# Linear attention followed by a gated MLP: w_in loaded and cast by tiles of 128 or 256 rows, new orders for the first two batches, one PSUM bank per transpose and kv, softmax of the next chunk spread over more units

## Chip, cores, metric

The kernel runs on one core of one Trainium2 chip. The metric is the device time of one execution in microseconds (us). Times quoted as medians come from several executions; profiles show one execution each, whose "span" is about 1.8 us shorter than its time. All executions named here are in the fast state unless said otherwise (slow means over 1.5% above the fastest execution of the same kernel; unknown, that there was a single one). A ratio is the mean time of one kernel's fast runs over that of the other's of the same rounds, so it is not quite the ratio of the medians quoted beside it.

Four engines matter: TensorE (PE in the profile, its weight loads PEld), VectorE (DVE), ScalarE (ACT) and GpSimd (POOL). In this kernel each works off its own list in the order of the program, and semaphores make it wait for the others. The order of the calls in the source is therefore the schedule.

## The reference

```python
# q, k, v: [8 batches, 8 heads, 576 tokens, 64]
q_s = softmax(q, axis=-1)                      # over the 64 features of a head
k_s = softmax(k, axis=2)                       # over the 576 tokens
kv  = einsum('bhsd,bhse->bhde', k_s, v)        # 64x64 per head
x   = einsum('bhsd,bhde->bhse', q_s, kv)       # -> [8*576, 512]
h   = x @ w_in                                 # w_in [512, 2048]
g   = h * sigmoid(beta * h)
out = g @ w_out                                # w_out [2048, 512]
```

## The kernel before

The tokens are worked on in nine chunks of 512: the first 512 tokens of each of the eight batches, and one chunk made of the eight tails of 64. A chunk has 16 "units" `j`, one for each 128 of the 2048 hidden columns. A unit is four h matmuls (one for each 128 rows of w_in, `kt`), a tanh on ScalarE, a multiply on VectorE that makes g, and four acc matmuls, all of 128x512. The attention of a batch is worked on in four pairs of heads. A pair has a kv (TensorE), a division by the sum of the exps of k (the "norm", VectorE, tile kvp), transposes of q (tp, copied to qsT), x (TensorE) and a copy of x as bfloat16 (xT). TensorE's results go to buffers called PSUM banks, and the program lets a bank be written again once its reader is done. While TensorE works on chunk n, the function `side` slips the softmax of chunk n+1 in between its units. The first two batches are ordered by hand, line by line.

```python
    EB = 2
    w_in_b = [const.tile([P, KT, 2 * P], BF16, name=f"w_in_b{hh}") for hh in range(2 * EB)]
    w_in_c = {blk: const.tile([P, KT, 4, P], BF16, name=f"w_in_c{blk}") for blk in range(EB, 4)}
    ...
    def w_cast(kind, blk, half, eng):              # float32 staging tile -> bf16
        t = wst[kind, blk]
        if kind == "in":
            if blk >= EB:                          # blocks 2 and 3: sorted while cast
                c = slice(2 * half, 2 * half + 2)
                evac(eng, w_in_c[blk][:, c], t[:, c, :].rearrange("p kt (q e) -> p kt e q", e=4))
                return
            dst = w_in_b[2 * blk + half][:]        # blocks 0 and 1: plain
            src = t[:, :, half * 256 : half * 256 + 256]
        ...
    def hpe(c, j, kts, tag="h"):                   # the h matmuls of unit j
        if (c, j) not in h_of:                     # a PSUM bank; "h" takes b2 and b3 in turn
            h_of[c, j] = ps.tile([P, MAIN], F32, tag=bank(tag), bufs=1, name=f"h{c}_{j}")
        ...
    def mm_a(c, j, tag=None):
        hpe(c, j, range(KT), tag or "h")
        th_act(c, j)
        g_dve(c, j)                                # frees the bank of h
```

Each partition reads two (blocks 0, 1) or four (blocks 2, 3) neighbouring rows of w_out, so unit j owns every second or every fourth column of w_in. In blocks 0 and 1 the weight load of TensorE picks every second column. In blocks 2 and 3 the cast does the picking: it reads a float32 every 16 bytes.

```python
    def side(n, u):                                # softmax of the next chunk, unit u
        ...
        o = 2 if n == 1 else 0
        if u in (2 + o, 3 + o):
            q_exp(qc, u - 2 - o)                   # ScalarE, one half of q
            q_sum(qc, u - 2 - o)                   # VectorE: row sum, reciprocal
        if u in (4 + o, 5 + o):
            q_mul(qc, u - 4 - o)                   # VectorE
            if kb < B:
                k_exp(kb, u - 4 - o)               # ScalarE
        ...
        if u == 6 + o:
            if kb < B:
                ktail_exp(kb)
            q_xbar(qc)                             # transpose by DMA
        ...                                        # kv at 9, x at 11 to 14
    for n in range(1, NCH):
        c = order[n]
        for j in range(LEAD if n == 1 else 0, NJ):
            if not (n > 1 and j == 3):
                mm_a(c, j, ...)
            if n > 1 and j == 2:
                mm_a(c, 3)                         # units 2 and 3 back to back
            ...
                mm_b(c, j - LAG)                   # acc matmuls two units later
            side(n, j)
```

(The start of batch 0, the loads and the stores are left out here.)

The softmax here doesn't subtract the row's maximum and nothing guards it: scores larger than these inputs give would overflow.

## Time and profile before

| | before |
|---|---|
| time, median of 4 runs | 287.56 us (287.34 to 288.11) |
| span of the profiled run | 285.8 us |
| TensorE busy | 277.2 us, 97% |
| first h matmul | 16.36 us |
| step from chunk to chunk | 29.51 us |

The kernel is bound by TensorE. In the steady part a 128x512 matmul starts every 0.216 us, the figure that the Trainium skill ("TensorE: Matmul & The Clock Gate", section "Wait — 56ns, not 53.3ns?") gives for a warm array, 215.7 ns. The timeline of TensorE shows the waits of the head. Columns: start and duration in us, engine, line, operation, output and inputs, count; in brackets the idle time before it and what ended it.

```profile
16.36 7.07 PE L420 MATMUL h<-xT,w_in_b 128*128 128x512 bf16 x31
23.27 3.62 PE L468 MATMUL acc<-w_out_b,g 128*128 128x512 bf16 x16
27.39 3.63 PE L420 MATMUL h<-xT,w_in_c 128*128 128x512 bf16 x16 [0.51 <-POOL w_in_c L162]
30.86 3.62 PE L468 MATMUL acc<-w_out_b,g 128*128 128x512 bf16 x15
34.70 3.63 PE L420 MATMUL h<-xT,w_in_c 128*128 128x512 bf16 x16 [0.22 <-DVE rq L238]
```

Sixteen matmuls at 0.216 us take 3.45 us, so from 23.27 the next group could start at 26.72, and from 30.86 at 34.31. It started at 27.39 and 34.70. The casts of w_in blocks 2 and 3 are in the timelines of ScalarE and GpSimd:

```profile
25.26 2.06 ACT L160 CAST w_in_c<-w_in 128x1024 bf16<-128x1024 f32 x1 [0.44 <-DMA w_in<-in_moe_w_in_dram]
25.29 2.05 POOL L162 CAST w_in_c<-w_in 128x1024 bf16<-128x1024 f32 x1 [2.94 <-DMA w_in<-in_moe_w_in_dram]
...
30.60 4.04 POOL L162 CAST w_in_c<-w_in 128x1024 bf16<-128x1024 f32 x2 [1.68 <-DMA w_in<-in_moe_w_in_dram]
```

They end at 27.34 and at 34.64. The second wait was put down to VectorE by the profile (the reciprocal that ended nearest), but the GpSimd cast ends just as near, and h reads its result. The costliest groups show how slow these casts are for their size:

```profile
L162 POOL CAST w_in_c<-w_in 128x1024 bf16<-128x1024 f32 x3 | 6.1, 2047 | 4.6 <-DMA w_in<-in_moe_w_in_dram 4.6
L162 POOL CAST w_out_b<-w_out 128x1024 bf16<-128x1024 f32 x6 | 6.2, 1041 | 3.2 <-DMA w_out<-in_moe_w_out_dram 3.2
```

The same number of elements on the same engine takes 2047 ns with a 16-byte step and 1041 ns without. "SBUF — State Buffer" in the Trainium skill (section "Door 1: The DMA port swizzle", the note on cachelines) says that a line is 16 bytes and that an access pays when it crosses to a new one; at a step of four float32 every access does. The trace agrees, on ScalarE too (2.06 against 1.03 us).

One stretch of the steady part, timeline of all engines (weight loads and transfers left out), shows a wait that I overlooked when I predicted:

```profile
83.55 1.22 DVE L237 TENSOR_REDUCE rq<-eq 128x16 f32<-128x1024 bf16 x1 [0.26 <-ACT eq L226]
84.47 0.69 ACT L430 ACTIVATE th<-h,beta_t 128x512 bf16<-128x512 f32 x1
84.97 1.16 DVE L237 TENSOR_REDUCE rq<-eq 128x16 f32<-128x1024 bf16 x1
...
86.00 1.03 PE L468 MATMUL acc<-w_out_b,g 128*128 128x512 bf16 x4
86.34 0.63 DVE L434 SCALAR_TENSOR_TENSOR g<-th,h 128x512 bf16<-128x512 bf16 x1
...
87.02 1.02 PE L420 MATMUL h<-xT,w_in_b 128*128 128x512 bf16 x4
```

The acc group at 86.00 should be followed by h at 86.86; h comes at 87.02, 0.16 us late, and the line shows no idle time because matmuls overlap in the trace. The h of unit 6 needs the bank of unit 4, which g of unit 4 frees. Its tanh was ready at 85.16, but VectorE did two row sums first and ended g at 86.97.

### The profile page before, as it was taken

To read this page: it belongs to the slowest core of one execution; us is meant where nothing else is said; L and a number is where in the kernel's file an instruction comes from. 1 tells how busy PE (TensorE), PEld (TensorE's weight loads), DVE (VectorE), ACT (ScalarE), POOL (GpSimd) and SP (SyncE) were. 2 spreads that over 40 slices of the span, in tenths; PEclk is the share of its full clock that TensorE was granted. 3 is DMA by queue.
4 is the path that set the end of the run, shared out by engine and by line. 5 is a ranking of instruction groups with operands and counts; after the bars stand their busy time and mean duration, and the time that the engine had idled before them with its cause. 6 is when DMAs were issued, how large, how long until landed. Compare 5 with 4: busy or idle time off the path is not lost.

```text
span 285.8 us, 4292 instructions
## 1 busy us (share of the span) xinstructions
PE 277.2 (97%) x1655; PEld 130.2 (46%) x1684; DVE 178.0 (62%) x279; ACT 164.3 (57%) x238; POOL 42.9 (15%) x58
## 2 busy tenths in 40 slices
PE   8799999999999999999999999999999999999995
PEld 3453445444444444444444444444445444445543
DVE  4863777595478457854694569546964596445361
ACT  4687773683486448734783468355934564554451
POOL 6445682120030012000300030002100000000000
PEclk9999999999999999999999999999999999999999
DMA  6999999908942973099219912796371033005003
GB/s 213 383 372 394 385 395 320 291 10 222 310 167 49 310 193 144 14 275 270 97 52 260 284 51 106 149 244 160 149 178 45 1 147 73 2 0 147 2 0 147
DMA packets 55760, 50.09 MB, mean 175 GB/s; under 512 B 26294, under 2 KB 49082, under 8 KB 55612
## 3 DMA queue, kind: packets, MB, share of 16 engines
q1 hardware_dynamic: 55596, 49.69, 57.5%
q8 instruction: 13, 0.21, 0.3%
q10 hardware_dynamic: 144, 0.13, 0.1%
q14 instruction: 7, 0.06, 0.1%
HBM read 36.71 MB, written 9.44 MB: 161 GB/s over the span
## 4 chain that ended last, share of the span: by engine, by line
PE 85%; DMA 9%; DVE 1%; SPq 1%; ACT 1%; issue 1%; POOL 0%
PE h L420 40%; PE acc L468 39%; DMA q_st<-in_q_dram 4%; DMA k_st<-in_k_dram 3%; DMA w_in<-in_moe_w_in_dram 3%; PE x L370 2%; PE kv L330 2%; PE acc L460 1%; SPq L115 1%; DVE g L434 1%; PE kv L289 1%; DVE rq L237 0%; POOL w_in_b L162 0%; ACT eq L226 0%; PE tp L274 0%
## 5 line engine op out<-in xcount | busy, mean ns | idle before, releaser
L434 DVE SCALAR_TENSOR_TENSOR g<-th,h 128x512 bf16<-128x512 bf16 x144 | 97.8, 683 | 87.4 <-ACT th L430 86.0
L430 ACT ACTIVATE th<-h,beta_t 128x512 bf16<-128x512 f32 x144 | 98.5, 688 | 93.4 <-PE h L420 90.8
L468 PE MATMUL acc<-w_out_b,g 128*128 128x512 bf16 x547 | 138.9, 379 | 0.6 <-issue 0.2
L468 PEld LDWEIGHTS <-g 128*128 128x128 bf16 x560 | 54.6, 98 | 65.5 <-DVE g L434 0.5
L420 PE MATMUL h<-xT,w_in_c 128*128 128x512 bf16 x280 | 71.8, 379 | 1.1 <-POOL w_in_c L162 0.5
L420 PE MATMUL h<-xT,w_in_b 128*128 128x512 bf16 x281 | 70.9, 379 | 0.6
L420 PEld LDWEIGHTS <-w_in_b 128*128 128x128 bf16 x288 | 28.1, 98 | 33.9 <-issue 1.6
L420 PEld LDWEIGHTS <-w_in_c 128*128 128x128 bf16 x288 | 27.2, 98 | 32.6 <-POOL w_in_c L162 1.7
L162 POOL CAST va<-v_st 128x576 bf16<-128x576 f32 (+1 forms) x14 | 18.6, 1328 | 145.7 <-DMA v_st<-in_v_dram 145.6
L237 DVE TENSOR_REDUCE rq<-eq 128x16 f32<-128x1024 bf16 x18 | 21.6, 1199 | 5.9 <-ACT eq L226 5.9
L243 DVE TENSOR_TENSOR eq<-eq,rq 128x1024 bf16<-128x1024 bf16 x18 | 22.2, 1235 | 0.1
L226 ACT ACTIVATE eq<-q_st 128x1024 bf16<-128x1024 f32 x16 | 16.3, 1049 | 5.2 <-DMA q_st<-in_q_dram 5.2
L160 ACT COPY o<-acc 128x512 f32<-128x512 f32 (+1 forms) x18 | 9.6, 575 | 8.9 <-PE acc L468 6.0
L162 DVE COPY o<-acc 128x512 f32<-128x512 f32 (+1 forms) x19 | 12.1, 670 | 3.4 <-PE acc L468 3.2
L162 DVE CAST xT<-x 128x512 bf16<-128x512 f32 x19 | 13.0, 685 | 0.7 <-PE x L370 0.7
L160 ACT CAST xT<-x 128x512 bf16<-128x512 f32 x17 | 9.9, 587 | 6.1 <-PE x L370 5.3
L181 ACT ACTIVATE ek<-k_st 128x1024 bf16<-128x1024 f32 x12 | 12.6, 1047 | 0.0
L370 PE MATMUL x<-qsT,kvp 128*128 128x512 bf16 x32 | 12.0, 380 | 0.0
L541 PE MATMUL warm<-kvp 128*128 128x512 bf16 x29 | 8.9, 468 | 1.2 <-DVE kvp L630 1.2
L162 POOL CAST w_in_c<-w_in 128x1024 bf16<-128x1024 f32 x3 | 6.1, 2047 | 4.6 <-DMA w_in<-in_moe_w_in_dram 4.6
L162 POOL CAST w_out_b<-w_out 128x1024 bf16<-128x1024 f32 x6 | 6.2, 1041 | 3.2 <-DMA w_out<-in_moe_w_out_dram 3.2
L174 ACT ACTIVATE ek<-k_st 128x576 bf16<-128x576 f32 x8 | 5.5, 681 | 2.0 <-DMA k_st<-in_k_dram 1.9
(49 smaller groups left out, 93.9 us busy)
## 6 DMA issues: line engine op xcount, KB each, us to landing
out_dram<-o SPq DMA_DIRECT2D x14, 512.0 KB, 3.4
q_st<-in_q_dram SPq DMA_DIRECT2D x6, 1024.0 KB, 6.8
k_st<-in_k_dram SPq DMA_DIRECT2D x6, 1024.0 KB, 7.6
v_st<-in_v_dram SPq DMA_DIRECT2D x6, 1024.0 KB, 11.0
k_st<-in_k_dram SPq DMA_DIRECT2D x8, 288.0 KB, 7.8
v_st<-in_v_dram SPq DMA_DIRECT2D x8, 288.0 KB, 7.5
q_st<-in_q_dram SPq DMA_DIRECT2D x4, 512.0 KB, 8.7
w_in<-in_moe_w_in_dram SPq DMA_DIRECT2D x4, 512.0 KB, 6.8
```

The costliest lines, as they stand in the source:

```text
L160: eng.copy(dst, src)
L162: eng.tensor_copy(dst, src)
L181: nc.scalar.activation(ek[b][:, :, h, :].rearrange("p i h d -> p h i d"), k_st[b][:, h, 0 : R * D].rearrange("p h (i d) -> p h i d", i=R), ...
L226: nc.scalar.activation(eq[b][:, :, s * m : (s + 1) * m, :].rearrange("p i h d -> p h i d"), q_st[b][:, s * m : (s + 1) * m, :].rearrange(" ...
L237: nc.vector.tensor_reduce(rq[b][:, 0, :, h], eq[b][:, :, h, :], axis=AX.X, op=ALU.add)
L243: eng.tensor_tensor(eq[b][:, :, h, :], eq[b][:, :, h, :], rq[b][:, 1, :, h].unsqueeze(3).to_broadcast((P, R, m, D)), ALU.mult,)
L370: nc.tensor.matmul(t[:], kvp[:, c, j, :], qsT[c][:, :, j, :])
L420: nc.tensor.matmul(h[:], w_in_u[j // 2][:, kt, j % 2, :] if j < 4 * EB else w_in_c[j // 4][:, kt, j % 4, :], x_of(c)[:, kt, :], start=(kt ...
L430: nc.scalar.activation(th[:], h_of[c, j][:], ACTF.Tanh, scale=beta_t[:, j : j + 1])
L434: nc.vector.scalar_tensor_tensor(out=g[:], in0=th_of.pop((c, j))[:], scalar=1.0, in1=h_of[c, j][:], op0=ALU.add, op1=ALU.mult)
L468: nc.tensor.matmul(acc[st][:], g[:, ds(st * P, P)], w_out_b[:, j, :], start=(j == 0), stop=(j == NJ - 1),)
L541: nc.tensor.matmul(t[:], kvp[:, B - 1, 0, :], kvp[:, B - 1, :, :].rearrange("p j r -> p (j r)"))
```

## The change

Its intent: let the first h matmuls start earlier and shorten the last chain of the attention of batch 0 (one PSUM bank per pair, casts split over two engines, beta early), cast w_in without the slow step, and spread the softmax of the next chunk so that it does not stand in front of tanh and g. The core of the diff, with cuts:

```diff
-    w_in_b = [const.tile([P, KT, 2 * P], BF16, name=f"w_in_b{hh}") for hh in range(2 * EB)]
-    w_in_c = {blk: const.tile([P, KT, 4, P], BF16, name=f"w_in_c{blk}") for blk in range(EB, 4)}
+    w_in_b = [
+        [const.tile([P, n, 4 * P], BF16, name=f"w_in_b{blk}_{i}") for i in range(KT // n)]
+        for blk, n in enumerate((1, 1, 1, 2))
+    ]
 ...
+    def w_unit(j, kt):
+        t = w_in_b[j // 4]
+        n = KT // len(t)
+        return t[kt // n][:, kt % n, :].rearrange("p (hh q e) -> p hh e q", hh=2, e=2)[:, j % 4 // 2, j % 2, :]
 ...
-    def vz_cast(b, j, eng, m=1):
+    def vz_cast(b, j, eng, m=1, part=None):        # part: 5/9 on GpSimd, 4/9 on ScalarE
 ...
-    def w_castk(blk, half, kh, eng):
-        c = slice(2 * kh, 2 * kh + 2)
-        evac(eng, w_in_b[2 * blk + half][:, c, :], wst["in", blk][:, c, half * 256 : half * 256 + 256])
+    def w_castk(blk, kt, eng):
+        evac(eng, w_in_b[blk][kt][:, 0, :], wst["in", blk][:, kt, :])
 ...                                               # loads of batch 0 in a new order, then
     w_load("in", 0, 0)                             # four row tiles of 256 KB, were two column halves
     w_load("in", 0, 1)
+    w_load("in", 0, 2)
+    w_load("in", 0, 3)
 ...                                               # both hand-written orders replaced, in side:
-        o = 2 if n == 1 else 0
-        if u in (2 + o, 3 + o):
-            q_exp(qc, u - 2 - o)
-            q_sum(qc, u - 2 - o)
-        if u in (4 + o, 5 + o):
-            q_mul(qc, u - 4 - o)
+        w = u
+        if w == 2:
+            q_exp(qc, 0)
+            q_sum(qc, 0)
+        if w == 3:
+            q_exp(qc, 1)
+        if w == 4:
+            q_sum(qc, 1)
             if kb < B:
-                k_exp(kb, u - 4 - o)
+                k_exp(kb, 0)
 ...
+        if w == 5:
+            q_mul(qc, 0)
             if kb < B:
                 ktail_exp(kb)
+        if w == 6:
+            if kb < B:
+                k_exp(kb, 1)
+        if w == 7:
+            q_mul(qc, 1)
             q_xbar(qc)
```

## The prediction

> **What bounds the kernel now.** TensorE. The busy table gives PE 277.2 of 285.8 us (97%), clock 0.999. In the timeline of chunks 2 to 7 a 128x512 matmul starts every 0.216 us (four in 0.86 us, as the Trainium skill's "TensorE: Matmul & The Clock Gate" states for a warm array, 215.7 ns), and the chain of waits repeats every 29.51 us with about 0.1 us of "issue". 128 h/acc matmuls, 4 x and 0.76 us of kv add to 29.2 us, so nothing is to be won there. Only the head can give: (a) the first h matmul starts at 16.36 us; until then PE has warm matmuls, waits and small attention work; (b) from 16.36 to 49.3 us (batch 0 done) the PE timeline shows gaps of 0.51 (waiting for the POOL cast of w_in_c), 0.22, 0.16 us and smaller, about 1.25 us against 31.7 us of work. The tail is not touched. The DMA engines are saturated (share 1.0 and more, 370 to 396 GB/s) from 5 to 45 us.
>
> **What the change does.**
> 1. w_in block 0 arrives in four 256 KB row tiles (about 0.7 us each at 380 GB/s) instead of two 512 KB column halves. The first half landed at 15.03 and its two casts (0.62 us) ended at 15.68. With the last v tile still landing at about 13.5, row tile 0 lands at about 14.2 and is cast by 14.9; kt 0 of four j runs at once, and each next tile brings 0.86 us of PE work per 0.7 us of DMA.
> 2. Each kv pair has its own bank, so pair 0's x is done early; the last pair's chain is v cast split over ACT and POOL (0.67 us to about 0.4), kv 0.45, norm 0.65, x, eviction 0.6. Beta's work leaves the end of this chain for the start, where its issue (0.3 to 0.4 us) should be absorbed.
> 3. w_in blocks 2 and 3: the old casts read with a 16-byte step, 2.05 us per 128x1024 on ACT and POOL, while w_out's contiguous ones take 1.04. "SBUF — State Buffer" (cachelines of 16 bytes) explains such a factor; the trace agrees. New ones should take 0.62 per 128x512: 3.5 us of engine time saved, on the path only as the 0.51 us gap. The de-interleaving moves to the weight loads, which took 98 ns both ways.
> 4. Batch 1: last loads are k and v instead of w_out; chained by hand, PE stays the bound until 47.7 us.
> 5. Softmax spread: PE did not wait for it; about 0, perhaps 0.2 us at the start of chunk 1.
>
> **Sum.** Start of h: about 1.1 us (8 h matmuls done by 16.95 instead of 18.1). Gaps of chunk 0: about 0.5 of 1.25. Chunk 1: 0.1. Total 1.7 us of 287.5.
>
> **Predicted 285.8 us, 80% range 284.6 to 287.2. Faster by over 2%: 0.02; within 2%: 0.965; slower by over 2%: 0.015.**
>
> **What would show it.** First h matmul at 14.7 to 15.3 us with x of pair 3 after it; no 2.05 us w_in casts; no gap at "POOL w_in" near 27 us; the acc matmuls of batch 0 end about 1.6 us earlier; chunk period unchanged at 29.5 us; tail unchanged.
>
> **What would make it wrong.** Landings of v and w_in that shift with the order; in-order blocking on ACT, where casts that wait for a landing stand before tanh; the DVE chain of three norms and two evictions holding up kt 1 and 2; batch-2 loads not landed when chunk 1, without its two-unit delay, wants them.

## The result

| | before | after |
|---|---|---|
| time, median of 4 runs | 287.56 us | 286.0 us (285.58 to 286.44) |
| ratio of fast runs | | 0.9943, 95% interval 0.9921 to 0.9966 |
| span of the profiled run | 285.8 us | 283.9 us |
| first h matmul | 16.36 us | 16.36 us |
| first acc matmul of batch 0 | 23.27 us | 23.48 us |
| h of units 8 and on, batch 0 | 27.39 us | 26.94 us |
| h of units 12 and on, batch 0 | 34.70 us | 33.84 us |
| batch 0 done, two h matmuls of chunk 1 done | 49.31 us | 48.45 us |
| double h group of chunk 2 | 79.96 us | 79.10 us |
| double h group of the last chunk | 256.25 us | 254.43 us |
| last 24 acc matmuls | 275.26 us | 273.44 us |

The predicted 285.8 us was 0.2 us off. But the rows of the table do not agree with the way in which it was reached. In these two profiles the start of h did not move; the head lost 0.21 us up to the first acc matmul (the x of the last pair, one matmul, now comes after the first three h matmuls and not before them), then won 1.07 us up to 33.84, then nothing more; and the steady part, from which nothing was expected, won 0.96 us between chunk 2 and the last chunk. One predicted sign is there only on its face: the acc matmuls of batch 0 end about 1.5 us earlier (47.8 instead of 49.3 us), but three matmuls of chunk 1 that used to come before the last of them now come after it. Like for like, the gain there is 0.86 us.

Timeline of TensorE, after:

```profile
16.36 0.81 PE L422 MATMUL h<-xT,w_in_b 128*128 128x512 bf16 x3
...
17.23 6.42 PE L422 MATMUL h<-xT,w_in_b 128*128 128x512 bf16 x29
23.48 3.62 PE L470 MATMUL acc<-w_out_b,g 128*128 128x512 bf16 x16
26.94 3.62 PE L422 MATMUL h<-xT,w_in_b 128*128 128x512 bf16 x16
...
33.84 1.03 PE L422 MATMUL h<-xT,w_in_b 128*128 128x512 bf16 x4
```

The first three h matmuls are followed by x of the last pair, then by the other 29. From 17.23 us on nothing waits: 23.48 plus 3.45 is 26.93. The casts, in the timeline of GpSimd, end well ahead of their readers:

```profile
24.91 0.61 POOL L158 CAST w_in_b<-w_in 128x512 bf16<-128x512 f32 x1 [0.17 <-DMA w_in<-in_moe_w_in_dram]
...
31.71 1.04 POOL L158 CAST w_in_b<-w_in 128x1024 bf16<-128x1024 f32 x1 [3.14 <-DMA w_in<-in_moe_w_in_dram]
```

And the stretch of the steady part, timeline of all engines, after. Now g of unit 4 stands between the two row sums (84.34), and h of unit 6 follows its acc group without a gap (85.14 plus 0.86 is 86.00):

```profile
82.69 1.22 DVE L234 TENSOR_REDUCE rq<-eq 128x16 f32<-128x1024 bf16 x1 [0.26 <-ACT eq L223]
...
84.34 0.69 DVE L436 SCALAR_TENSOR_TENSOR g<-th,h 128x512 bf16<-128x512 bf16 x1
84.94 1.21 DVE L234 TENSOR_REDUCE rq<-eq 128x16 f32<-128x1024 bf16 x1
85.14 1.03 PE L470 MATMUL acc<-w_out_b,g 128*128 128x512 bf16 x4
...
86.01 1.03 PE L422 MATMUL h<-xT,w_in_b 128*128 128x512 bf16 x4
```

The chain of waits of the profile after, in order of time, says what the first h matmul waited for (start, duration, what):

```profile
2.12 5.64 DMA v_st<-in_v_dram
...
9.54 0.75 PE warm L543 x3
...
10.55 0.76 DVE qsT L158 x2
11.34 1.23 DVE rq L234
...
13.39 1.21 DVE eq L240
...
15.64 0.24 DVE kvp L304
15.92 0.60 PE x L370 x2
```

It starts with the landing of the first v tile, goes through the first kv, beta's transposes and three dummy matmuls ("warm") on TensorE, and from 10.55 us on it lies on VectorE, up to x and h. It is not w_in: the first row tile of w_in was cast by about 15.5 us.

### The profile page after: what moved, and what is told of

It reads as the page before. It is cut to its first block, busy times and chain, and to the rows that moved or that the text cites. A ratio compares the mean times of both kernels' runs of the same rounds, so it can differ in the third digit from the quotient of the medians.

```text
span 283.9 us, 4325 instructions
## 1 busy us (share of the span) xinstructions
PE 278.1 (98%) x1683; PEld 130.5 (46%) x1683; DVE 179.6 (63%) x285; ACT 164.4 (58%) x241; POOL 37.8 (13%) x59
## 4 chain that ended last, share of the span: by engine, by line
PE 94%; DMA 2%; DVE 2%; SPq 0%; POOL 0%; issue 0%; ACT 0%; POOLq 0%
PE h L422 44%; PE acc L470 43%; PE x L370 2%; DMA v_st<-in_v_dram 2%; PE kv L330 2%; PE acc L462 1%; PE kv L289 1%; DVE rq L234 0%; DVE eq L240 0%; PE tp L270 0%; PE x L374 0%; DVE kvp L304 0%; POOL va L158 0%; DVE qsT L158 0%; PE warm L543 0%
## 5 line engine op out<-in xcount | busy, mean ns | idle before, releaser
L422 PE MATMUL h<-xT,w_in_b 128*128 128x512 bf16 x576 | 144.0, 379 | 0.0
L470 PE MATMUL acc<-w_out_b,g 128*128 128x512 bf16 x560 | 140.8, 379 | 0.0
L422 PEld LDWEIGHTS <-w_in_b 128*128 128x128 bf16 x576 | 55.5, 98 | 63.9
L158 POOL CAST va<-v_st 128x320 bf16<-128x320 f32 (+2 forms) x14 | 16.7, 1192 | 150.0 <-DMA v_st<-in_v_dram 150.0
L543 PE MATMUL warm<-kvp 128*128 128x512 bf16 x33 | 10.3, 465 | 1.2 <-DVE kvp L627 1.2
L158 POOL CAST w_in_b<-w_in 128x512 bf16<-128x512 f32 (+1 forms) x11 | 6.9, 650 | 6.4 <-DMA w_in<-in_moe_w_in_dram 6.4
L543 PEld LDWEIGHTS <-kvp 128*128 128x128 bf16 x33 | 3.6, 116 | 6.4 <-issue 3.6
L330 PEld LDWEIGHTS <-ek 128*64 128x64 bf16 x192 | 4.1, 111 | 2.5 <-ACT th L432 2.5
L363 DVE TENSOR_TENSOR kvp<-kv,rk 64x256 bf16<-64x256 f32 x12 | 5.1, 422 | 0.3
## 6 DMA issues: line engine op xcount, KB each, us to landing
v_st<-in_v_dram SPq DMA_DIRECT2D x6, 1024.0 KB, 10.7
```

The source lines that it names most:

```text
L158: eng.tensor_copy(dst, src)
L422: nc.tensor.matmul(h[:], w_unit(j, kt), x_of(c)[:, kt, :], start=(kt == 0), stop=(kt == KT - 1),)
L470: nc.tensor.matmul(acc[st][:], g[:, ds(st * P, P)], w_out_b[:, j, :], start=(j == 0), stop=(j == NJ - 1),)
L543: nc.tensor.matmul(t[:], kvp[:, B - 1, 0, :], kvp[:, B - 1, :, :].rearrange("p j r -> p (j r)"))
```

## The experiments

Three theories follow from this. C: the slow casts caused both waits of the head. S: the two row sums in a row cost 0.16 us in each of six chunks. V: the head waits for the VectorE chain. The rival of C is that the new orders and banks gave the gain (O), the rival of S is the prediction (P).

### Softmax placement put back, and alone

The changed kernel with the body of `side` of the old one, and the reverse:

```diff
# e1_new_old_side: in the changed kernel (shortened; compare the diff above)
-        if w == 2: ... q_exp(qc, 0), q_sum(qc, 0)
-        ...
-        if w == 7: ... q_mul(qc, 1), q_xbar(qc)
+        o = 2 if n == 1 else 0
+        if u in (2 + o, 3 + o): ... q_exp, q_sum
+        ...
+        if u == 6 + o: ... ktail_exp, q_xbar
# e2_old_new_side: the reverse, in the old kernel
```

> The changed kernel with the old placement of the next chunk's softmax put back. Theory S (the spread of the softmax takes away a wait of 0.16 us in each of chunks 2 to 7, where the second row sum stands before g of unit 4 on VectorE and holds back the bank of h of unit 6): the step from chunk to chunk goes from 29.35 back to 29.51 us, the first 48 us stay, the span grows from 283.9 by about 1.0 to 284.9 us. Rival P (the prediction on record: TensorE did not wait for the softmax): span within 0.2 us of 283.9.

Measured: 286.9 us (median of 6), ratio to the old kernel 0.9974 (0.996 to 0.9987), profiled span 284.8 us. The double h groups of chunks 2 and 3, timeline of TensorE:

```profile
78.99 1.89 PE L422 MATMUL h<-xT,w_in_b 128*128 128x512 bf16 x8
108.51 1.89 PE L422 MATMUL h<-xT,w_in_b 128*128 128x512 bf16 x8
```

The step is back to 29.51 us (29.52 between these two rounded starts, 29.51 between the next), and the head is as in the changed kernel (first h at 16.26). S is right, P is wrong.

> The old kernel with only the new placement of the softmax. Theory S: chunk step 29.35 us instead of 29.51, span 285.8 - 1.0 = 284.8 us, with the first 49 us unchanged. Rival P: 285.6 to 285.8 us.

Measured: 286.35 us, ratio 0.9962 (0.9942 to 0.9981). The profiled span is only 285.4 us, but that profile is of one of the two longest of its six executions (287.18 us, still a fast run), and its head ran 0.58 us later than the old kernel's. The steps are what was to be tested:

```profile
80.54 1.89 PE L420 MATMUL h<-xT,w_in_b 128*128 128x512 bf16 x8
109.89 1.89 PE L420 MATMUL h<-xT,w_in_b 128*128 128x512 bf16 x8
```

The step is 29.35 us, and from chunk 2 to the last chunk 175.33 us (80.54 to 255.87) against 176.29 us before. The placement gives the 0.96 us by itself.

### Which half of the placement

Only the VectorE part, and only the ScalarE part, in the old kernel (one run each, so their state is unknown and their times are not compared):

```diff
# e3_old_dve_part
-            q_sum(qc, u - 2 - o)
-        if u in (4 + o, 5 + o):
-            q_mul(qc, u - 4 - o)
+        if u in (2 + o, 4 + o):
+            q_sum(qc, (u - 2 - o) // 2)
+        if u in (5 + o, 7 + o):
+            q_mul(qc, (u - 5 - o) // 2)
# and q_xbar at 7 + o instead of 6 + o
# e4_old_act_part
-            if kb < B:
-                k_exp(kb, u - 4 - o)
+        if u in (4 + o, 6 + o):
+            if kb < B:
+                k_exp(kb, (u - 4 - o) // 2)
# and ktail_exp at 5 + o instead of 6 + o
```

> The old kernel with only the VectorE half of the new placement: second row sum two units after the first, multiplies at units 5 and 7, transpose at 7; the exps of k on ScalarE stay. If the wait is VectorE's (g of unit 4 behind the second row sum), the chunk step falls from 29.51 to 29.35 us. If it was ScalarE's (tanh behind four exps), it stays at 29.51.

> The old kernel with only the ScalarE half: the second exp of k two units after the first, the tail's exp between them; the row sums and multiplies on VectorE stay. VectorE theory: chunk step stays at 29.51 us. ScalarE theory: 29.35 us.

Measured: steps of 29.35 us in the first (83.96 to 113.31 us) and 29.51 us in the second (80.38 to 109.89). The wait was VectorE's alone. (The first kernel moves the multiplies and the transpose too. That the row sum is what counted is read from the profile of before: only it stands in the list between the tanh and g of unit 4.) But the first kernel took 290.6 us, longer than before, for a reason that I had not expected. Its timeline of TensorE in chunk 1:

```profile
68.76 1.03 PE L468 MATMUL acc<-w_out_b,g 128*128 128x512 bf16 x4
72.74 0.38 PE L370 MATMUL x<-qsT,kvp 128*128 128x512 bf16 x1 [2.96 <-DMA qsT<-eq]
```

I had kept the old delay of two units in chunk 1 (`o`), so the transpose by DMA was issued at unit 9, after the last multiply, and x of unit 11 waited for it. The transpose took 5.4 us from issue to landing in that chunk. The changed kernel drops the delay, which is why it can multiply as late as unit 7. A part of a change that looks idle can be what makes another part harmless.

The second kernel showed something else about the old casts:

```profile
27.68 3.63 PE L420 MATMUL h<-xT,w_in_c 128*128 128x512 bf16 x16 [1.33 <-POOL w_in_c L162]
```

Here h had started at 15.64 us, 0.7 earlier than in the profile of before, and TensorE simply waited longer (1.33 us instead of 0.51) for the cast. With the slow casts the start of h is not what sets the pace of the head.

### Contiguous casts alone, and both parts together

```diff
# e5_old_contig: in the old kernel
-    EB = 2
+    EB = 4                                # all blocks laid out as blocks 0 and 1
-    beta_q = const.tile([4 - EB, 4 * P], F32, name="beta_q")
-    nc.sync.dma_start(beta_q[:], ...)     # and its four small transposes and its copy
# e6_old_contig_new_side: the same, and the new body of side
```

> The old kernel with w_in blocks 2 and 3 cast without the 16-byte step (and w_out and beta laid out to match), its orders and its loads of w_in kept. Theory C (the slow casts alone caused both waits of TensorE near 27 and 34.5 us): the casts of 128x1024 take about 1.05 us instead of 2.05; the first h matmul stays at 16.3 to 16.4 us; the h groups that started at 27.39 and 34.70 us start at about 26.9 and 33.8; span about 0.9 shorter, 284.9 us. Rival O (the new orders and banks of the head gave the gain): the waits change only by 0.5 us or less in all, span 285.3 or more.

Measured: 286.18 us, ratio 0.9952 (0.994 to 0.9965), span 284.4 us. The timeline of GpSimd and that of TensorE:

```profile
24.97 1.04 POOL L161 CAST w_in_b<-w_in 128x1024 bf16<-128x1024 f32 x1 [2.95 <-DMA w_in<-in_moe_w_in_dram]
...
30.25 2.03 POOL L161 CAST w_in_b<-w_in 128x1024 bf16<-128x1024 f32 x2 [1.67 <-DMA w_in<-in_moe_w_in_dram]
```

```profile
15.81 7.07 PE L419 MATMUL h<-xT,w_in_b 128*128 128x512 bf16 x32
...
26.17 3.62 PE L419 MATMUL h<-xT,w_in_b 128*128 128x512 bf16 x16
...
33.08 3.62 PE L419 MATMUL h<-xT,w_in_b 128*128 128x512 bf16 x16
```

Both waits are gone, with the old orders kept: h of units 8 and 12 starts 10.36 and 17.27 us after the first h matmul, against 11.03 and 18.34 us before, and 10.35 and 17.26 us are what 48 and 80 matmuls take at 0.2157 us. The edit also changes the layout of w_out and beta, but the arithmetic leaves no room for that: with casts of 2.05 and 4.04 us from 24.97 and 30.25 us on, h would have waited until 27.0 and 34.3 us and not started at 26.17 and 33.08. C is right and O is wrong about them. The start of h also moved, by 0.55 us, which was not expected: part of it may be that beta now needs two small transposes instead of six between x of pairs 2 and 3, part the spread of starts described below; this run does not separate them.

> The old kernel with both: contiguous casts and the new placement of the softmax; old head, old loads of w_in. If theories C and S are the whole of the change, it reaches the changed kernel: span 283.9 us (0.9 + 1.0 less than 285.8), and the new orders of batches 0 and 1, the row tiles and the banks are worth nothing or a little less than nothing. Rival O: it stays 0.7 us or more above the changed kernel's 283.9.

Measured: 285.53 us, ratio 0.9921 (0.9908 to 0.9934), span 283.7 us, first h at 15.20 us. The old kernel with two small edits reaches the changed one. Repeated on another chip:

> The old kernel with contiguous casts and the new softmax placement, again. If the new orders of batches 0 and 1, the row tiles and the banks are worth nothing (theory C + S is the whole of the gain), it stays within 0.3 us of the changed kernel of this call. If they are worth the 1.1 us that the prediction gave to the start of h, it is 1 us slower.

Measured: 285.49 us, ratio 0.9934 (0.9914 to 0.9953), span 283.6 us. The changed kernel of the same rounds was 1.33 us slower (286.82 us, see next), so "within 0.3 us" was missed, on the side that speaks against the new head.

### The changed kernel again, and what its new head does

> The changed kernel itself, unchanged, beside the others on one chip and with more rounds. Ratio to the old kernel 0.994 to 0.995 (285.9 to 286.2 us); in the profile the first h matmul at 16.2 to 16.5 us, chunk step 29.35 us, no idle piece of TensorE ahead of h after 17.3 us.

Measured: 285.58 us, ratio 0.9935 (0.9918 to 0.9952), span 283.3 us, first acc matmul at 22.64 us, step 29.35 us. The first h matmul came earlier than expected: at 15.72 us in the records, at about 15.5 us in fact, since one of the three has no record. The chain of waits ahead of it is another one than in the first profile:

```profile
5.34 7.41 DMA v_st<-in_v_dram
...
12.81 0.84 POOL va L158
```

Here a landing of v and its cast on GpSimd came last, then kv, x and h on TensorE, and no row sum of VectorE. Which chain ends last changes between executions of one kernel.

> The changed kernel once more, as the measure for the other three on the same chip: 285.6 to 286.1 us, first h matmul at 15.7 to 16.4 us (three profiles so far: 16.36, 16.26, 15.72).

Measured: 286.82 us (285.74 to 287.49), ratio 0.9972 (0.9948 to 0.9996), span 285.5 us, first acc matmul at 25.05 us: 1.57 us later than in the first profile of the same kernel, and outside what I had expected. The timeline of TensorE and a line of the table of windows (us, then busy time and count for each engine, the granted clock, the DMA share, GB/s) show why:

```profile
9.17 0.48 PE L289 MATMUL kv<-va,ek 64*64 64x65 bf16 x18 [2.62 <-POOL va L158]
...
12.15 2.86 PE L543 MATMUL warm<-kvp 128*128 128x512 bf16 x8
```

```profile
12.00:14.00 2.00, 2.00 (x6) 0.73 (x5) 1.97 (x4) 1.15 (x3) 0.82 (x2) 0.50 1.00 365
```

In this execution the opening dummies ended earlier (6.55 instead of 7.58 us) and the first v tile landed later (its cast began at 8.57 instead of 7.79 us), so that TensorE stood idle for 2.62 us (1.15 us in the first profile). From 10.7 to 14.1 us its granted clock was 0.50. The eight "warm" matmuls, dummies that are there to keep the clock up, then took 2.86 us instead of 1.89 and stood in front of the real kv of pair 2. The new head puts the first kv, which needs v, ahead of the transposes, which do not, and so exposes TensorE to this landing; in the seven profiles with the old head the wait in front of the first kv was at most 1.33 us. Of the six executions of that set three more took over 286.3 us with a clock of 1.0 in the records; no profile shows why.

Two more tries at the head. First another start, in the changed kernel:

```diff
# e7_new_head
-    load_q(0, 2, 1)                       # was fifth
+    load_q(0, 2, 1)                       # third; beta loaded near the end of batch 0
-    kvz_mm(0, 0, "acc3", 1)
-    q_mul(0, 0)
-    beta_pe("acc2"); beta_ev(); kvz_norm(0, 0)
-    q_exp(0, 1)
-    ... tpe(0, 0), tpe(0, 1), q_ev, q_ev, ..., q_sum(0, 1), ..., xev(0, 0, V)
+    q_mul(0, 0)
+    tpe(0, 0, "acc2"); tpe(0, 1, "acc1")
+    q_exp(0, 1)
+    ... q_ev, q_ev, q_sum(0, 1), ..., kvz_mm(0, 0), kvz_norm(0, 0), q_mul(0, 1), ..., xev(0, 0, A)
+    ... beta_pe, beta_ev at the end
```

> The changed kernel with another start for batch 0: second half of q loaded third instead of fifth, beta loaded late and its transposes and copy moved to the end of the attention part, the first transposes on TensorE ahead of the first kv, one eviction of x moved from VectorE to ScalarE. Theory V (in the changed kernel the first h matmul waits for the VectorE chain of evictions, row sum, multiply and norms that starts only when the exp of the second half of q ends at 10.6 us; not for w_in): that exp starts at about 8.4 instead of 9.64 us, the norm of pair 1 ends near 14.7 instead of 15.87, the first h matmul is at 15.0 to 15.5 instead of 16.36 us, span about 0.9 shorter, 283.0 us. Rival W (the landings of v and w_in set the start): first h within 0.3 us of 16.36, span 283.6 or more.

Measured: 285.67 us, ratio of the five fast runs 0.9931 (0.9915 to 0.9948), no better than the changed kernel of the same rounds. The profiled execution took 591.36 us: the 128x512 matmuls ran at less than half speed from start to end (mean 680 ns instead of 379, and four in 1.89 us instead of 0.86), while the records of the clock say 1.0. It is left out, and the kernel was run again.

> The changed kernel with the other start of batch 0, run again because its profile fell into an execution with a TensorE at half speed. Its five other times, median 285.6, were no better than the changed kernel's 285.6. Theory V still says: first h matmul at 15.0 to 15.5 us. If that is so and the time is the same, the start was given back at a later wait for w_in or w_out, which the profile must show between 17 and 45 us. If first h is at 15.7 or later, theory V fails at the start itself.

Measured: 285.68 us (285.31 to 285.81), ratio 0.9934 (0.9918 to 0.995), span 283.5 us. From the timeline of all engines:

```profile
7.72 1.06 ACT L223 ACTIVATE eq<-q_st 128x1024 bf16<-128x1024 f32 x1 [1.45 <-DMA q_st<-in_q_dram]
...
14.80 0.17 DVE L301 RECIPROCAL rk<-kv 128x1 f32<-128x1 f32 x1 [0.63 <-PE kv L289]
...
15.52 0.61 PE L370 MATMUL x<-qsT,kvp 128*128 128x512 bf16 x2 [0.47 <-DVE kvp L304]
16.18 0.59 PE L422 MATMUL h<-xT,w_in_b 128*128 128x512 bf16 x2
```

The exp moved 1.92 us earlier, but x of pair 1 only 0.40 us (15.92 to 15.52), less than it differs between two profiles of the changed kernel itself (15.06 in the second). VectorE now has a hole in front of the norm of pair 1, waiting for its kv. (One of the three h matmuls ahead of x has no record, so the first is about 0.2 us earlier than the line says, near 15.96.) By the bound, 15.7 us, V fails at the start itself. The chain of waits of this profile says why:

```profile
12.20 0.86 PE warm L543 x4
...
14.02 0.21 PE tb L576
```

It is TensorE's own list: four dummies, the kv of pair 2, eight transposes of q and beta's two stood ahead of the kv of pair 1, which began at 14.28 us although its v had been cast by 13.70. V named what was last in the first profile of the changed kernel, but taking it away brought at most 0.4 us, because a chain on another engine lies close behind.

Then the loads of w_in block 0 in two halves instead of four tiles:

```diff
# e8_new_two_loads
-            c = slice(0, KT) if half is None else slice(half, half + 1) if blk == 0 else slice(2 * half, 2 * half + 2)
+            c = slice(0, KT) if half is None else slice(2 * half, 2 * half + 2)
-    w_load("in", 0, 2)
-    w_load("in", 0, 3)
```

> The changed kernel with w_in block 0 loaded as two 512 KB halves of two row tiles each instead of four 256 KB tiles; casts and all orders kept. If the small loads let h start earlier, as the prediction had it, the first h matmul moves 0.3 to 0.7 us later and the span with it. If h waits for the attention chain instead, nothing moves: first h within the spread of the changed kernel, time within 0.2 us of it.

Measured: 285.76 us, ratio 0.9937 (0.9919 to 0.9956), first acc matmul at 23.69 us, which lies within the changed kernel's own 22.64 to 25.05. From the timeline of all engines:

```profile
16.13 0.60 PE L370 MATMUL x<-qsT,kvp 128*128 128x512 bf16 x2 [0.21 <-DVE kvp L304]
```

The first tile was cast 0.5 us later than with four loads (by about 16.0 us), and TensorE still waited for the norm of pair 1, not for w_in; the first h matmul, one more without a record, was at about 16.57 us. The small loads are worth nothing that these runs can show.

## Why the prediction was right, and where it was not

The time was right, the steps were right only in part. Against the sum (1.1 + 0.5 + 0.1 us) the start of h came out 1.3 us worse (0.21 us lost instead of 1.1 us won), the casts 0.6 us better (1.07 instead of 0.5) and the softmax 0.96 us better (instead of about 0). That these errors nearly cancelled was luck. One by one:

- Start of h, predicted -1.1 us: wrong. In the first pair of profiles the first h matmul stayed at 16.36 us and the first acc matmul came 0.21 us later. Starts vary from execution to execution: the first acc matmul lies at 22.73 to 23.99 us in four profiles with the old head and the slow casts, at 22.22 to 22.72 in three with the old head and contiguous casts, and at 22.64 to 25.05 in four with the new head. The failed step is "the first h matmul at 14.7 to 15.3". I chained the landing of v3 (predicted 13.5, its cast began at 13.80 us) and of w_in (cast predicted by 14.9, done by about 15.5 us), but treated VectorE as free. In the profile VectorE begins the second row sum at 11.34 us, behind two evictions that wait for TensorE, and its norms end at 15.87 and 16.56. In the second profile the landing and cast of v came last, with the other start TensorE's own list, so VectorE is one of several limits within about half a microsecond. Moving the head's pieces further (the other start, the two loads) won nothing, and the old head with contiguous casts did as well (285.53 and 285.49 us). "Absorbed" was also too kind to the early beta: in the profile after, ScalarE sat idle for 1.38 us until beta's transposes were done, with the second exp of q next in its list.
- The v cast split over two engines, predicted 0.4 us: for the last pair the GpSimd part took 1.08 us, because VectorE's multiply ran at the same time; alone such a part took 0.46 us. In all six profiles of the new head and its variants such a cast ended 0.32 us after the multiply. The Trainium skill ("SBUF — State Buffer", "Who interferes with whom") says that GpSimd and a VectorE instruction with two SBUF inputs lock each other out when the GpSimd one reads SBUF; the trace agrees. In the first profile nothing on the chain waited for it, but in the second the 0.84 us cast on the chain is one of these.
- Slow casts, predicted 3.5 us of engine time and about 0.5 us of the path: mechanism right, size too small. The head won 1.07 us between the first acc matmul and unit 12, since the wait at 34.70 us, which the profile put down to VectorE, was the same cast. The old orders with contiguous casts have neither wait.
- Batch 1: right. TensorE stayed the bound to 48.45 us, against 47.7 by hand.
- Softmax spread, predicted about 0: wrong. It gave 0.96 us, six times 0.16, shown by putting it back and by moving it alone; the row sums on VectorE are the cause, not the exps (the halves were run once each; which VectorE piece it is was read from the trace). The failed step is "nothing is to be won there" for a step of 29.51 us against a sum of 29.2. I let the 0.3 us between them pass because the chain showed no wait and only about 0.1 us of "issue"; six steps make that nearly 2 us, and half of it was a wait that could be taken away.
- Tail unchanged: right (the last 24 acc matmuls begin 1.82 us earlier, the span ends 1.9 us earlier).

What stays open: what the new orders of batch 0 and 1 and the banks are worth by themselves. The two-edit kernel also has one beta load and four transposes fewer than the old one, and its start of h (15.20 us, and 15.31 in the repeat) is partly that. All that is shown is that the changed kernel's head does not beat it. Open too is what made three of the longer executions of the changed kernel long, and the spread of the starts itself.

## What to carry to other kernels

When a steady period is longer than the sum of its instructions, find the instruction that starts late by comparing starts, not idle times: a 0.16 us wait hides under overlapping matmuls and is paid in every period. When a wait is put down to one engine, look for another instruction that ends at the same moment and whose result is read there. And before hoping for an earlier start, walk the whole chain in program order on every engine, and check that no later gate, like a slow cast, would take the gain back.

## What the Trainium skill lacked or had wrong

- "GPSIMD Engine Reference", "Performance pitfalls for Q7 kernels", gives about +50% for reading with a byte step over 8. Here a float32 to bf16 cast with a 16-byte step took 2047 ns against 1041 ns on GpSimd, +97%.
- No page says that ScalarE pays the same: 2.06 us against 1.03 us for 128x1024. The 16-byte cacheline note in "SBUF — State Buffer" would explain it but gives no duration.
- "TensorE: Matmul & The Clock Gate" gives an idle window of about 3.4 us before the clock halves. Here the clock fell to 0.50 from 10.7 to 14.1 us in an execution whose longest idle stretch was 2.62 us and had ended 1.5 us before; where the longest was 1.52 us (the kernel with two loads) it stayed at 1.0. Whether the short work in between counted is not shown.
- No page describes an execution that runs at less than half speed from start to end while the clock records say 1.0: one of twelve of the kernel with the other start, 591.36 us, four 128x512 matmuls in 1.89 us instead of 0.86. (The nearest is the warning on unreliable clock events in "TensorE: Matmul & The Clock Gate".)
